# Sixteen small VectorE operations for f, layer-one roots behind the sine, a new priority table and last adds on GpSimd in a two-layer state-space kernel

## The chip, the cores and the metric

The kernel runs on one core of a Trainium2 chip. The metric is device microseconds (us) of one execution. Times are medians of several executions. A ratio is the mean time of one kernel's runs over the mean of the other's runs of the same rounds, so it is not quite the ratio of the medians that stand beside it. Each run of an altered kernel was timed beside fresh runs of the kernel before on the same chip; those medians lay between 357.3 and 358.5 us.

## The reference, cut to what matters

```python
x = A_x                                   # 2048 tokens x 640
for layer in (1, 2):                      # the same weights both times
    x = x + A(layernorm(x))               # diagonal complex recurrence h = lam*h + B u, y = 2 Re(C h) + D u
    x = x + B(layernorm(x))               # layernorm(x) times a long convolution of k and v (by FFT in the reference)
```

In A, `lam = exp(dt * Lambda)` and `B_bar = f * B` with `f = (lam - 1) / Lambda`, all complex, 640 states. The B term's convolution depends on k, v and fixed weights alone, so it can be computed at any time before it is used.

## The kernel before: the parts that the argument touches

The 2048 tokens are worked in four chunks of 512; a chunk has four quarters of 128 tokens ("q"). A layer-A chunk passes layernorm (its root is on ScalarE), products (`bp`), a rotation by a table of sines and cosines (`ri`, VectorE), a scan, the rotation back (`ro`), and four large groups of products (`cp`), one for each quarter.

The program does not fix an order by hand. Each piece of work is a task with dependencies, an estimated duration and a rank from a table `WHEN`. A list scheduler in the program gives each engine, as soon as it is free, the ready task of lowest rank (for some tasks the second number says how long to wait for the first choice of engine), and the instructions are then emitted in that planned sequence. Each engine runs its sequence strictly in order, so a planned order that does not fit the real durations shows up as waiting. The plan is made anew for every program.

The sine table of the rotation, and who must be done before it:

```python
B = (aw["tab"][...first 640*5 elements...], aw["W1"][:, 0])   # B's real part lies in the table's memory
...
t_m = S.add(f"a_gm{k}", "pe", ..., [t_dd] + w0s + bms, e_gm)     # five products that read B; gms = all five
...
def e_t1(_):                                                     # ScalarE: the table
    nc.scalar.activation(aw["tab"][:, 2], st["r"], ACT.Sin, ...)
    nc.scalar.activation(ab, st["r"], ACT.Abs)
    nc.scalar.activation(aw["tab"][:, 1], ab, ACT.Sin, ...)
    for j in range(NJ):
        nc.scalar.activation(aw["rtab"][:, j, :], st["it"], ACT.Identity, scale=0.0, bias=...)
t_t1 = S.add("a_t1", "act", 6.7, [t_t0] + gms, e_t1)             # so the sine waits for gms
```

The layer-one roots (in `bn_stats`) and the end of layer B in its last chunk, a group per quarter:

```python
t_sd = S.add(name + "_sd", "act", ..., [t_bn], e_sd)             # Sqrt: another activation table than Sin
...
# last chunk, one quarter q:
e_u:  b = (x + nmean) * Y          # one fused VectorE operation; needs only the mean
e_m:  Y = b * rstd + x             # one fused VectorE operation; needs the root
# other chunks: e_u normalizes (ScalarE or VectorE), one product over four quarters, four adds on VectorE
```

Of the kernel before, what the change touches and what calls it, by code (L numbers as in the profile page):

```python
# [9 lines left out]
ALU = mybir.AluOpType  # L10
# [7 lines left out]
P = 128  # L18
L = 2048
D = 640  # L20
# [32 lines left out]
    "warm": -5, "yt_io0": 2.55, "yt_ph0": 4.27, "yt_sin0": 5.89, "yt_neg0": 9.88, "yt_io6": 132.6, "yt_ph6": 8.2, "yt_sin6": 9.91, "yt_neg6": 13.01,  # L53
    "yt_io12": 8.8, "yt_ph12": 11.54, "yt_sin12": 13.59, "yt_neg12": 16.53, "yt_Ci": 21.14, "yt_Si": 22.8, "yt_nsi": 30.27, "yt_f0": 1.22, "yt_f2": 6.07,
    "yt_f3": 8.4, "yt_f4": 9.65, "yt_h0": 0.07, "yt_h1": 0.97, "yt_h2": 5.13, "yt_h3": 9.63, "kv_dsl": 1.97, "kv_kd": 2.73, "kv_k0": 13.36, "kv_k1":
    14.32, "kv_k2": 14.97, "kv_d0": 5.67, "kv_d1": 6.57, "kv_d2": 10.23, "kv_ds0": 10.65, "kv_lk0": -0, "kv_lv0": 9.8, "kv_mm0:0": 12.25, "kv_ev0:0":
    15.4, "kv_mm0:1": 15.02, "kv_ev0:1": 17.2, "kv_st0": 21.1, "kv_ds1": 13.44, "kv_lk1": 12.55, "kv_lv1": 15, "kv_mm1:0": 21.79, "kv_ev1:0": 25.02,
    "kv_mm1:1": 20.06, "kv_ev1:1": 22.17, "kv_st1": 32.7, "kv_ds2": 18.01, "kv_lk2": 35.6, "kv_lv2": 40.3, "kv_mm2:0": 48.16, "kv_ev2:0": 52.03,
    "kv_mm2:1": 40.92, "kv_ev2:1": 50.79, "kv_st2": 54.8, "kv_ds3": 30.92, "kv_lk3": 47.3, "kv_lv3": 43.8, "kv_mm3:0": 54.17, "kv_ev3:0": 56.25,
    "kv_mm3:1": 57.88, "kv_ev3:1": 59.99, "kv_st3": 76.1, "kv_ds4": 55.32, "kv_lk4": 68.7, "kv_lv4": 72.6, "kv_mm4:0": 78.97, "kv_ev4:0": 81.57,  # L60
    "kv_mm4:1": 72.36, "kv_ev4:1": 77.61, "kv_st4": 85.5, "a_pl": 0.17, "a_p0": 11.24, "a_p1": 13.98, "a_p2": 14.63, "a_p3": 15.78, "a_p4": 18.43, "a_p5":
    20.56, "a_p6": 23.36, "a_lamd": 23.86, "a_f": 28.37, "a_dd": 16.07, "a_ldB0": 2.4, "a_ldB1": 7.4, "a_wl00:0": 34.4, "a_wl00:1": 31.5, "a_wc00:0":
    37.93, "a_wm00:0": 39.1, "a_wc00:1": 40.53, "a_wm00:1": 40.04, "a_wl01:0": 40.21, "a_wl01:1": 37.9, "a_wc01:0": 42.58, "a_wm01:0": 49.98, "a_wc01:1":
    51.1, "a_wm01:1": 53.25, "a_wl02:0": 46.1, "a_wl02:1": 42.6, "a_wc02:0": 48.69, "a_wm02:0": 54.03, "a_wc02:1": 55.37, "a_wm02:1": 58.88, "a_wl03:0":
    71.4, "a_wl03:1": 56.5, "a_wc03:0": 74.94, "a_wm03:0": 75.97, "a_wc03:1": 76.97, "a_wm03:1": 79.87, "a_wl04:0": 65.2, "a_wl04:1": 74.9, "a_wc04:0":
    78.59, "a_wm04:0": 80.65, "a_wc04:1": 81.65, "a_wm04:1": 82.89, "a_b00:0": 9.82, "a_b0e0:0": (10.51, 0), "a_b00:1": 8.06, "a_b0e0:1": (9.33, 3),
    "a_b00:2": 11.53, "a_b0e0:2": (13.01, 1.5), "a_b00:3": 10.63, "a_b0e0:3": (12.42, -1), "a_b00:4": 7.7, "a_b0e0:4": (8.75, 3), "a_b01:0": 49.89,
    "a_b0e1:0": (50.52, 3), "a_b01:1": 14.62, "a_b0e1:1": (17.28, 0.8), "a_b01:2": 23.8, "a_b0e1:2": (24.94, 3), "a_b01:3": 18.33, "a_b0e1:3": (19.59,
    -1), "a_b01:4": 23.52, "a_b0e1:4": (24.36, 1.5), "a_b10:0": 33.92, "a_b1e0:0": (35, 3), "a_b10:1": 32.55, "a_b1e0:1": (33.68, 0), "a_b10:2": 25.31,
    "a_b1e0:2": (26.42, -1), "a_b10:3": 29.77, "a_b1e0:3": (31.02, 0), "a_b10:4": 26.8, "a_b1e0:4": (28.17, 3), "a_b11:0": 42.65, "a_b1e1:0": (43.58, -1),  # L70
    "a_b11:1": 28.31, "a_b1e1:1": (29.65, -1), "a_b11:2": 34.63, "a_b1e1:2": (35.54, -1), "a_b11:3": 46.77, "a_b1e1:3": (48.11, 99), "a_b11:4": 30.56,
    "a_b1e1:4": (31.47, -1), "a_gm0": 84.5, "a_ge0": (87.86, -1), "a_gm1": 87.84, "a_ge1": 90.96, "a_gm2": 104.18, "a_ge2": (107.4, 0), "a_gm3": 98.47,
    "a_ge3": (115.43, 1.5), "a_gm4": 92.78, "a_ge4": 96.07, "a_wl10:0": 97.9, "a_wl10:1": 89.8, "a_wc10:0": 115.48, "a_wm10:0": 107.45, "a_wc10:1":
    111.58, "a_wm10:1": 112.92, "a_wl11:0": 101.84, "a_wl11:1": 103.04, "a_wc11:0": 106.68, "a_wm11:0": 109.36, "a_wc11:1": 121.12, "a_wm11:1": 122.95,
    "a_wl12:0": 116.24, "a_wl12:1": 117.44, "a_wc12:0": 121.91, "a_wm12:0": 132.45, "a_wc12:1": 135.94, "a_wm12:1": 138.06, "a_wl13:0": 131.59,
    "a_wl13:1": 130.39, "a_wc13:0": 137.56, "a_wm13:0": 138.85, "a_wc13:1": 139.99, "a_wm13:1": 141.05, "a_wl14:0": 144.12, "a_wl14:1": 142.92,
    "a_wc14:0": 148.92, "a_wm14:0": 150.68, "a_wc14:1": 153.82, "a_wm14:1": 157.45, "a_ti": 20.17, "a_ta": 22.96, "a_t0": 26.17, "a_t1": 122.82, "a_t2":
    131.25, "yq0_kl": 4.8, "yq0_ka": 15.17, "yq0_KA:m0": 16.75, "yq0_KA:e0": (18.76, -1), "yq0_KA:m1": 19.31, "yq0_KA:e1": 20.32, "yq0_KA:m2": 17.03,
    "yq0_KA:e2": (17.86, -1), "yq0_KA:m3": 18.61, "yq0_KA:e3": (19.66, 99), "yq0_KB:m0": 25.89, "yq0_KB:e0": (27.01, 99), "yq0_KB:m1": 27.38, "yq0_KB:e1":
    (28.75, 0.8), "yq0_KB:m2": 24.08, "yq0_KB:e2": (25.52, 1.5), "yq0_KB:m3": 28.87, "yq0_KB:e3": (30.31, 0), "yq0_KB:m4": 26.57, "yq0_KB:e4": 27.91,  # L80
    "yq0_vl": 26.3, "yq0_VA:m0": 31.92, "yq0_VA:e0": (32.55, 0), "yq0_VA:m1": 31.61, "yq0_VA:e1": (32.24, 6), "yq0_VA:m2": 32.27, "yq0_VA:e2": (33.15,
    0.8), "yq0_VA:m3": 33.47, "yq0_VA:e3": (34.1, 99), "yq0_VB:m0": 35.91, "yq0_VB:e0": 36.98, "yq0_VB:m1": 37.48, "yq0_VB:e1": (38.73, 99), "yq0_VB:m2":
    36.58, "yq0_VB:e2": (37.97, 0), "yq0_VB:m3": 38.79, "yq0_VB:e3": (41.58, 0), "yq0_VB:m4": 40.18, "yq0_VB:e4": (39.51, 1.5), "yq1_kl": 28.99, "yq1_ka":
    34.59, "yq1_KA:m0": 39.9, "yq1_KA:e0": (41.76, 1.5), "yq1_KA:m1": 35.29, "yq1_KA:e1": (35.98, 6), "yq1_KA:m2": 35.57, "yq1_KA:e2": 36.58, "yq1_KA:m3":
    38.6, "yq1_KA:e3": (39.71, 0.8), "yq1_KB:m0": 43.29, "yq1_KB:e0": (44.32, 3), "yq1_KB:m1": 45.76, "yq1_KB:e1": (47.02, 0), "yq1_KB:m2": 44.86,
    "yq1_KB:e2": 46.12, "yq1_KB:m3": 43.97, "yq1_KB:e3": 45.22, "yq1_KB:m4": 47.51, "yq1_KB:e4": 49.78, "yq0_pw": 42.46, "yq0_IB:m0": 52.34, "yq0_IB:e0":
    53.78, "yq0_IB:m1": 51.44, "yq0_IB:e1": (52.78, 99), "yq0_IB:m2": 50.27, "yq0_IB:e2": (51.82, 0), "yq0_IB:m3": 53.95, "yq0_IB:e3": (54.47, 3),
    "yq0_IB:m4": 53.05, "yq0_IB:e4": 54.88, "yq0_tt": 64.47, "yq1_vl": 49.69, "yq1_VA:m0": 56, "yq1_VA:e0": (56.63, -1), "yq1_VA:m1": 57.69, "yq1_VA:e1":
    (58.43, 3), "yq1_VA:m2": 56.43, "yq1_VA:e2": (57.53, 3), "yq1_VA:m3": 56.75, "yq1_VA:e3": (57.6, -1), "yq1_VB:m0": 59.7, "yq1_VB:e0": 60.79,
    "yq1_VB:m1": 61.49, "yq1_VB:e1": (62.75, 0.8), "yq1_VB:m2": 60.37, "yq1_VB:e2": (61.69, 0.8), "yq1_VB:m3": 62.39, "yq1_VB:e3": 63.65, "yq1_VB:m4":  # L90
    61.27, "yq1_VB:e4": (62.15, -1), "yq0_IA:m0": 65.54, "yq0_IA:e0": (66.37, 6), "yq0_IA:m1": 66.03, "yq0_IA:e1": (67.27, 0.8), "yq0_st": 69.05,
    "yq2_kl": 52.2, "yq2_ka": 58.65, "yq2_KA:m0": 64.22, "yq2_KA:e0": (65.38, -1), "yq2_KA:m1": 63.55, "yq2_KA:e1": (64.19, -1), "yq2_KA:m2": 64.8,
    "yq2_KA:e2": (65.43, -1), "yq2_KA:m3": 63.86, "yq2_KA:e3": (64.49, 6), "yq2_KB:m0": 68.05, "yq2_KB:e0": (69.33, 99), "yq2_KB:m1": 66.86, "yq2_KB:e1":
    (68.17, 1.5), "yq2_KB:m2": 68.73, "yq2_KB:e2": (70.23, 0.8), "yq2_KB:m3": 69.62, "yq2_KB:e3": (71.13, 1.5), "yq2_KB:m4": 67.83, "yq2_KB:e4": (69.07,
    1.5), "yq1_pw": 66.59, "yq1_IB:m0": 78.02, "yq1_IB:e0": (79.4, -1), "yq1_IB:m1": 74.47, "yq1_IB:e1": (75.77, 0), "yq1_IB:m2": 76.21, "yq1_IB:e2":
    (77.78, 0.8), "yq1_IB:m3": 77.12, "yq1_IB:e3": (78.82, -1), "yq1_IB:m4": 75.54, "yq1_IB:e4": (76.67, 3), "yq1_tt": 80.49, "yq2_vl": 64.11,
    "yq2_VA:m0": 74.09, "yq2_VA:e0": (74.72, 0), "yq2_VA:m1": 71.61, "yq2_VA:e1": 72.94, "yq2_VA:m2": 71.25, "yq2_VA:e2": (73.84, 3), "yq2_VA:m3": 70.96,
# [312 lines left out]
def a_setup_tasks(S, nc, wp, St, consts, t_go, A_Lambda_re, A_Lambda_im, A_B_re, A_B_im, A_C_re, A_C_im, A_log_dt, A_Dskip, after_sin):  # L410
# [240 lines left out]
    def e_t2(_):  # L651
# [5 lines left out]
        v.tensor_scalar(aw["ctab"][:, 2, :], st["sn"][:, 1, :], -1.0, None, ALU.mult)  # L657

    T["tab"] = [S.add("a_t2", "dve", 1.2, [t_t1], e_t2)]

    T["w"] = w0s + w1s + gs
    return aw, T, t

# [879 lines left out]
```

## Time and profile before

| | kernel before |
|---|---|
| median | 358.4 us |
| profiled span | 356.8 us |
| TensorE busy, VectorE busy, ScalarE busy | 327.5, 315.1, 256.4 us |
| TensorE idle before its last product (345.7 us) | 18.2 us, of it 17.1 before 142 us |
| from TensorE's last product to the end | 11.1 us |
| stretches at half the TensorE clock before its end | one, 36.8 to 40.3 us |

The trace's clock records give TensorE's granted clock in stretches that are multiples of 3.41 us; the clock takes the values 1.0 and 0.5. ScalarE in order of time (start, length, engine, line, operation, then out and in), in the kernel before:

```profile
102.85 1.28 ACT L712 ACT_TABLE_LOAD   x1
104.15 0.30 ACT L712 ACTIVATE std<-mv,eps 128x4 f32<-128x4 f32 x1
...
107.94 0.92 ACT L726 ACTIVATE b<-b,nmr,rstd 128x640 bf16<-128x640 bf16 x1
...
126.65 1.28 ACT L644 ACT_TABLE_LOAD   x1
...
131.83 2.11 ACT L648 ACTIVATE rtab<-b,s_r 128x258 f32<-128x258 f32 x5
```

Chunk 0's root is at 104 us. The table with its load holds ScalarE from 126.65 to 133.85.

### The profile page before, as it was taken

What the parts mean: (1) busy time and instruction counts of PE and PEld (TensorE: products, weight loads), DVE (VectorE), ACT (ScalarE), POOL (GpSimd) and SP (SyncE); (2) the same over time, 40 slices, a digit from 0 to 9 for tenths busy, and PEclk for the clock granted to TensorE, in tenths of its full rate; (3) what the DMA queues carried; (4) which work ended last, traced back from release to release, by engine and by line L of the source; (5) the groups of instructions that cost most, each with busy time, mean ns of one, the idle gap of its engine ahead of it and who ended that gap; (6) DMA issues with size and microseconds to landing.
All of it is one profiled execution on the core that took longest, in us unless ns stands there. A gap on an engine that the chain in (4) does not pass through costs nothing.

```text
span 356.8 us, 8409 instructions
## 1 busy us (share of the span) xinstructions
PE 327.5 (92%) x3534; PEld 247.6 (69%) x3565; DVE 315.1 (88%) x479; ACT 256.4 (72%) x406; POOL 20.8 (6%) x51
## 2 busy tenths in 40 slices
PE   7686998989998997999999999999999999999970
PEld 7346876867686986986685677686866767755640
DVE  8799798798799797999999969979999679999896
ACT  3999798898799999943378599797256577306850
POOL 5841003000000000000000000000000000000000
PEclk9999899999999999999999999999999999999996
DMA  7999999999999982790226690605032022220141
GB/s 193 208 235 188 182 184 217 193 186 202 237 245 163 184 174 46 144 233 2 62 73 119 137 333 34 147 18 132 0 68 81 3 16 59 75 75 2 50 172 73
DMA packets 118712, 45.91 MB, mean 129 GB/s; under 512 B 111629, under 2 KB 112914, under 8 KB 118674
## 3 DMA queue, kind: packets, MB, share of 16 engines
q1 hardware_dynamic: 118528, 45.36, 59.9%
q8 instruction: 28, 0.46, 0.5%
q14 instruction: 10, 0.08, 0.1%
q10 hardware_dynamic: 146, 0.01, 0.0%
HBM read 17.38 MB, written 7.86 MB: 71 GB/s over the span
## 4 chain that ended last, share of the span: by engine, by line
PE 69%; ACT 10%; DVE 8%; DMA 7%; issue 3%; SPq 2%; DVEq 0%; ACTq 0%
PE ps L859 31%; PE ps L770 11%; PE ps L773 11%; ACT b L382 6%; PE ps L608 3%; PE ps L1163 3%; DMA b<-in_A_C_im_dram 2%; DMA b<-in_B_v_dram 2%; DVE b L1169 2%; PE ps L1313 2%; DMA b<-b 2%; PE ps L1314 1%; PE ps L1208 1%; SPq L536 1%; DMA b<-in_B_k_dram 1%
## 5 line engine op out<-in xcount | busy, mean ns | idle before, releaser
L382 ACT ACTIVATE b<-ps 128x1024 bf16<-128x1024 f32 (+3 forms) x125 | 109.6, 945 | 29.5 <-PE ps L773 25.5
L859 PEld LDWEIGHTS <-b 128*128 128x128 bf16 x880 | 67.7, 98 | 48.3
L859 PE MATMUL ps<-W,b 128*128 128x128 bf16 (+1 forms) x629 | 95.7, 298 | 0.6
L770 PE MATMUL ps<-b,BT 128*128 128x256 bf16 x400 | 56.8, 273 | 0.0
L773 PE MATMUL ps<-b,BT 128*128 128x256 bf16 x400 | 56.7, 273 | 0.0
L808 DVE TENSOR_TENSOR_SCAN b<-rtab,b 128x1290 bf16<-128x1290 f32 x16 | 44.7, 2833 | 0.3
L773 PEld LDWEIGHTS <-BT 128*128 128x128 bf16 x400 | 39.1, 98 | 4.5
L770 PEld LDWEIGHTS <-BT 128*128 128x128 bf16 x400 | 38.6, 98 | 4.4
L726 ACT ACTIVATE b<-b,nmr,rstd 128x640 bf16<-128x640 f32 (+1 forms) x43 | 37.0, 915 | 6.2 <-DVE nmr L693 6.2
L681 ACT ACTIVATE junk<-b,nmean 128x640 bf16<-128x640 f32 x48 | 39.7, 828 | 1.5
L1232 PE MATMUL ps<-b,b 128*128 128x128 bf16 x170 | 35.1, 219 | 1.2 <-ACT G L382 0.7
L1235 PE MATMUL ps<-b,b 128*128 128x128 bf16 x170 | 35.4, 219 | 0.0
L1237 PE MATMUL ps<-b,b 128*128 128x128 bf16 x150 | 32.8, 219 | 0.0
L1234 PE MATMUL ps<-b,b 128*128 128x128 bf16 x150 | 32.8, 219 | 0.0
L384 DVE CAST b<-ps 128x1024 bf16<-128x1024 f32 (+2 forms) x24 | 26.2, 1109 | 6.3 <-PE ps L1208 2.7
L867 ACT ACTIVATE b<-ps 128x640 f32<-128x640 f32 x16 | 11.1, 697 | 22.8 <-PE ps L859 22.8
L859 PE MATMUL ps<-G,b 128*128 128x128 bf16 (+1 forms) x152 | 26.5, 295 | 0.4
L1163 PE MATMUL ps<-b,fd 128*128 128x512 bf16 x73 | 18.6, 380 | 3.8 <-POOL fd L1141 2.0
L1313 PE MATMUL ps<-b,b 128*128 128x128 bf16 x160 | 19.4, 219 | 2.6 <-ACT b L382 2.1
L1314 PE MATMUL ps<-b,b 128*128 128x128 bf16 x160 | 19.2, 219 | 0.0
L552 ACT ACTIVATE b<-b,s_F 128x640 f32<-128x640 bf16 x20 | 17.2, 859 | 1.8 <-DVE W L556 1.4
L556 DVE SCALAR_TENSOR_TENSOR W<-b,s_F 128x640 bf16<-128x640 bf16 x20 | 17.4, 882 | 1.0 <-ACT b L552 0.7
(210 smaller groups left out, 560.3 us busy)
## 6 DMA issues: line engine op xcount, KB each, us to landing
b<-in_A_x_dram SPq DMA_DIRECT2D x8, 640.0 KB, 4.9
b<-ysd SPq DMA_DIRECT2D x8, 640.0 KB, 5.1
b<-in_B_ssm_k_dram SPq DMA_DIRECT2D x5, 512.0 KB, 8.6
kvd<-b SPq DMA_DIRECT2D x5, 512.0 KB, 4.3
b<-kvd SPq DMA_DIRECT2D x5, 512.0 KB, 5.4
ysd<-b SPq DMA_DIRECT2D x5, 512.0 KB, 5.0
out_dram<-b SPq DMA_DIRECT2D x8, 320.0 KB, 2.2
tab<-in_A_B_re_dram SPq DMA_DIRECT2D x1, 800.0 KB, 7.4
```

What stands on the lines that cost most here:

```text
L382: nc.scalar.activation(out, in_, ACT.Copy)
L681: nc.scalar.activation(small.junk, src(q), ACT.Square, bias=st["nmean"][:, i:i + 1], scale=1.0, accum_out=st["ssq"][:, i:i + 1])
L726: nc.scalar.activation(dst, src, ACT.Identity, bias=st["nmr"][:, i:i + 1], scale=st["rstd"][:, i:i + 1])
L770: nc.tensor.matmul(pb[:, jj, c2, :], lhsT=aw["BT1"][:, c2, j, k, :], rhs=uT[:, 0:2, k, :], start=(k == 0), stop=False)
L773: nc.tensor.matmul(pb[:, jj, c2, :], lhsT=aw["BT0"][:, c2, k, j * P:(j + 1) * P], rhs=uT[:, 2:4, k, :], start=False, stop=(k == NJ - 1))
L808: nc.vector.tensor_tensor_scan(gv, rt, gv, 0.0, ALU.mult, ALU.add)
L859: nc.tensor.matmul(pc[:, o0:o1], lhsT=lh, rhs=rh, start=(n == 0), stop=(n == len(ops) - 1))
L1163: nc.tensor.matmul(pk[:, 512 * b:512 * (b + 1)], lhsT=s_ds.get()[:, l, :], rhs=kT[:, t0:t0 + 512], start=(l == 0), stop=(l == 3))
L1232: nc.tensor.matmul(ps[:, g, 0, :], lhsT=T["Cf"].get()[:, q, :], rhs=are, start=True, stop=single)
L1234: nc.tensor.matmul(ps[:, g, 0, :], lhsT=T["Sf"].get()[:, q, :], rhs=A[:, 2 * q + 1, :], start=False, stop=True)
L1235: nc.tensor.matmul(ps[:, g, 1, :], lhsT=T["NSf"].get()[:, q, :], rhs=are, start=True, stop=single)
L1237: nc.tensor.matmul(ps[:, g, 1, :], lhsT=T["Cf"].get()[:, q, :], rhs=A[:, 2 * q + 1, :], start=False, stop=True)
```

## The change

Its intent: fewer tiny dependent operations for f; one activation-table load fewer for the roots and none for the sine, by making the roots follow the sine; a tail in which GpSimd and ScalarE take work from VectorE; and a new priority table for all of that. Cut to its core:

```diff
 WHEN = {
-    (862 ranks)
+    (every one of them new)
 }
@@ f: 25 small VectorE operations become 16 on pairs of planes; lam is stored as (-im, re, im)
@@ the table and the layer-one roots
+    T["t1"] = [t_t1]
-def bn_stats(S, nc, small, src, x_ready, name, uses):
+def bn_stats(S, nc, small, src, x_ready, name, uses, after):          # after = T["t1"]
-    t_sd = S.add(name + "_sd", "act", ..., [t_bn], e_sd)
+    t_sd = S.add(name + "_sd", "act", ..., [t_bn] + after, e_sd)
@@ layer B, last chunk
-            if len(qs) == 1:                 # every quarter in the fused form
+            if qs[0] == 3:                   # only quarter 3 in the fused form
...
+                    engs, ests = (("dve", "pool"), (0.77, 1.4)) if out is not None and c >= NCH - 2 else ...   # adds on either engine
+        if len(groups) > 1:                  # a store per quarter in the last chunk
```

## The prediction

> **What bounds the kernel now.** I read the page's busy row first, then the busy time by stretch, then the chain of waits and the order of time in the last stretch.
>
> The busy row has TensorE at 92% of 356.8 us and VectorE at 88%. Such shares are averages, so I cut the span where the behaviour changes. The columns are the stretch, its length, busy us (instructions) of TensorE, its weight loads, VectorE, ScalarE and GpSimd, then the granted clock, the DMA share and GB/s.
>
> ```profile
> 0.00:30.00 30.00, 22.02 (x240) 16.61 (x243) 25.16 (x71) 24.25 (x38) 17.83 (x45) 1.00 0.98 212
> 30.00:60.00 30.00, 27.43 (x395) 22.75 (x395) 25.94 (x48) 26.68 (x36) 2.94 (x6) 0.94 1.04 196
> 60.00:100.00 40.00, 37.28 (x559) 28.91 (x562) 32.38 (x33) 34.08 (x41) 0.00 (x0) 1.00 1.10 210
> 100.00:142.00 42.00, 38.16 (x550) 33.00 (x549) 36.47 (x74) 41.47 (x54) 0.00 (x0) 1.00 0.90 154
> 142.00:345.80 203.80, 202.65 (x1803) 146.35 (x1820) 187.43 (x244) 128.52 (x237) 0.00 (x0) 1.00 0.35 86
> 345.80:357.00 11.20, 0.00 (x0) 0.00 (x0) 7.69 (x13) 1.42 (x4) 0.00 (x0) 0.73 0.29 117
> ```
>
> There are three regimes. A head, 0 to 142 us, in which TensorE idles 8.0 + 2.6 + 2.7 + 3.8 = 17.1 us; in its last 42 us ScalarE is busy for 41.5, so the head ends ScalarE-bound. A body of 203.8 us in which TensorE idles only 1.2 us: it sets the pace and nothing else matters. A tail of 11.0 us, 345.8 to the span's end at 356.8, without any TensorE work. The change removes no matrix product, so it can gain only from those 17.1 us and those 11.0 us.
>
> The tail in order of time (start, length, what):
>
> ```profile
> 345.89 0.81 DVE L871 SCALAR_TENSOR_TENSOR b<-ps,b 128x640 f32<-128x640 f32 x1
> 346.63 0.88 DVE L901 SCALAR_TENSOR_TENSOR b<-b,nmean,b 128x640 bf16<-128x640 f32 x1
> 346.75 0.20 ACT L676 ACTIVATE nmean<-sums 128x1 f32<-128x1 f32 x1 [2.74 <-DVE b L871]
> 346.99 0.83 ACT L681 ACTIVATE junk<-b,nmean 128x640 bf16<-128x640 f32 x1
> 347.55 0.89 DVE L905 SCALAR_TENSOR_TENSOR b<-b,rstd,b 128x640 bf16<-128x640 bf16 x1
> 347.72 0.19 ACT L681 ACTIVATION_READ_ACCUMULATOR junk<-b,nmean 128x1 f32 x1
> 347.94 0.29 ACT L686 ACTIVATE std<-ssq,eps 128x1 f32<-128x1 f32 x1
> 348.35 2.47 DVE L901 SCALAR_TENSOR_TENSOR b<-b,nmean,b 128x640 bf16<-128x640 f32 x3
> 350.86 1.68 DVE L905 SCALAR_TENSOR_TENSOR b<-b,rstd,b 128x640 bf16<-128x640 bf16 x2
> 352.45 0.16 DVE L691 RECIPROCAL rstd<-std 128x1 f32<-128x1 f32 x1
> ...
> 352.72 0.88 DVE L905 SCALAR_TENSOR_TENSOR b<-b,rstd,b 128x640 bf16<-128x640 bf16 x1
> ```
>
> ScalarE has the root of the last quarter at 348.23, but VectorE takes up its reciprocal only at 352.45: for 4.2 us the last quarter waits behind work of other quarters. VectorE's backlog sets the end, not the dependency. After 353.6 there remain 3.2 us of output store.
>
> ScalarE's part of the head, as the page's group shows it: roots (L712) and the table's sine (L644) evict each other's activation table.
>
> ```profile
> L712 ACT ACT_TABLE_LOAD  x2: 1283/1283/1283, 102.9 to 134.9; - x2
> L644 ACT ACT_TABLE_LOAD  x1: 1283/1283/1283, 126.7 to 126.7; - x1
> ```
>
> So: load, two roots, load, sine, load, remaining roots. And one group about GpSimd (ns min/median/max):
>
> ```profile
> L1141 POOL TENSOR_TENSOR fd<-ident_bf,skf x20: 392/394/2311, 12.5 to 55.7; 128x128 bf16<-128x128 bf16 x20
> L487 DVE TENSOR_TENSOR b<-ident_bf,s_lam x1: 2311/2311/2311, 25.5 to 25.5; 128x1920 bf16<-128x1920 bf16 x1
> ```
>
> A 394 ns GpSimd product once took 2311 ns, exactly the length of the VectorE product beside it.
>
> **What the Trainium skill says.** (1) "ScalarE: Activation LUTs", What ACT_TABLE_LOAD costs: about 1283 ns per switch plus a drain of about 1380. The trace agrees on 1283; the drain does not show (the load starts at 102.85, the root behind it at 104.15), so I count 1.28. (2) "SBUF — State Buffer", Who interferes with whom: a VectorE instruction with two SBUF inputs and a GpSimd instruction that reads SBUF exclude each other for the whole instruction. The 2311 ns above agrees. (3) "GPSIMD Engine Reference", 3.1 Elementwise: about 2.6 cycles per element for two inputs, at 1.2 GHz 2.17 ns. With the trace's 394 ns for 128 columns the fixed part is 394 - 277 = 117, so 640 columns give an estimate of 1.5 us, against 0.77 on VectorE. No run shows that form yet. (4) "DMA: Bandwidth & Descriptors", Anatomy of one DMA: a fixed 2 us, mostly the receipt. The 320 KB output stores land after 2.2 us, so halving one saves little.
>
> **The change, part by part.**
>
> *f.* I count 25 operations before (lines 496 to 525), not 29, and 16 after. They run from 31.12 to 34.26 us: a dependent step costs 0.20 us, an independent one about 0.08. The new sequence has nine dependent steps and six others: 9 x 0.20 + 6 x 0.08 = 2.3 against 3.1, so 0.8 us of VectorE. Its first reader is the weight scaling at 42.2 us, 8 us later: slack, and of the 0.8 us I give the end 0.1. The new order of lam has the same three operations: 0.
>
> *Roots behind the sine.* One root load in place of two, and the sine's own falls away since the last set loaded is the sine's: 2 x 1.28 = 2.6 us less on ScalarE between 100 and 142 us, where it is full. The ceiling is TensorE's idle time there, 3.8 us. TensorE has other work to take up (the other layer's transforms), and the first two chunks' roots, at 104 and 108 us before, now wait for the table, which waits for all five products of the setup. I expect under half to arrive: 1.0.
>
> *The order.* Nearly every priority is new. Both loads of B now come first, and four of the five B_im transposes move from later into the first stretch, where TensorE idles 8 us. Five products of 128 columns at the trace's 0.056 us spacing make 0.28 us each, 1.1 for four. But the first kv product then starts later, behind 1.6 MB of B. I give this 0.4.
>
> *Tail.* Before, between 337.85 and 353.6 us, VectorE runs nearly without a gap. Concerned are four adds of chunk 2 (0.77 each) and, for quarters 0 to 2 of chunk 3, two fused operations (0.82 + 0.85): 3.1 + 5.0 = 8.1 us. After: a product per quarter, from 1.49 us for four quarters about 0.45; a normalization, on ScalarE or 0.57 on VectorE; an add, on either of VectorE and GpSimd. My choice: four of seven adds on GpSimd, two of three normalizations on ScalarE. VectorE keeps 3 x 0.77 + 3 x 0.45 + 0.57 = 4.2, a relief of 3.9 us. Against it the exclusion: four adds of 1.5 us on GpSimd, each able to hold up a two-input VectorE operation for part of its length; I take 0.4 us each, 1.6 back. Net 2.3. The floor: the last quarter's own chain (root out at 348.23, reciprocal, product with 1/std and add to 349.5, store 3.1) would end at 352.6, which caps the gain at 4.2. The last store is 160 KB in place of 320: 0.1.
>
> Sum: 0.1 + 1.0 + 0.4 + 2.3 + 0.1 = 3.9 us. From the median 358.4 that is 354.5.
>
> **The rivals.** *The GpSimd adds give back what they take.* For it: the 2311 ns record, and that GpSimd is twice slower by the estimate. If all four meet a two-input VectorE operation, 2.8 us come back, and a last add on GpSimd at 1.5 us could itself be last. Tail gain about 1, time 356.3. Against it: accumulating reads from PSUM[...] have one SBUF input and pass freely, and the very last quarter keeps its VectorE form. *The head is bound by DMA.* The DMA share is 0.9 to 1.1 up to 142 us and the chain there contains transposes of C and of the activations (3 to 5 us each); then freeing ScalarE moves nothing, and the later roots delay the first chunk: head gain -1 to 0, time about 356. Against it: ScalarE has hardly a gap from 110 to 142 us. *The new order is much better.* If it closes half of the head's 17.1 us besides the tail, 358.4 - 8 - 3 = 347. Against it: 6 to 8 us of that idle time are start-up and dependencies that no order removes, and the kernel was already tuned the same way.
>
> **Range and chances.** From -0.8 (both pessimistic rivals) to -7 (the tail at its cap and 3 us from the head): 351.5 to 357.6 at 8 in 10. Faster by over 2% means below 351.2, that is 7.2 us: the cap of 4.2 and 3 us from the head: 0.11. Slower by over 2% needs a new long wait in the body: 0.02. Within: 0.87.
>
> **What would show it.** One L712 table load and none at L644, four loads in all instead of six. TensorE idle in the body still about 1 us; if it is 3 or more, the new order has cost something and I am wrong there. The distance from TensorE's last product to the end: 8.6 us in place of 11.0; if still about 11, look at GpSimd adds above 1.5 us and VectorE operations stretched beside them. TensorE's last product near 344.3 in place of 345.7; if it is unchanged, the head's gain was an illusion, and if below 342, I undervalued the order.

## The result, and the profile after

| | before | after |
|---|---|---|
| median | 358.51 us (4 runs, 358.19 to 359.01) | 381.60 us (4 runs, 380.71 to 382.58) |
| ratio | | 1.064, 95% interval 1.061 to 1.067 |
| profiled span, mean clock | 356.8, 0.987 | 379.5, 0.964 |
| TensorE's last product ends | 345.7 | 368.6 |
| from there to the end | 11.1 | 10.9 |
| activation-table loads | 6 | 4 |

The table loads are as intended, and the tail is as long as it was. All the loss, 22.9 us, is before TensorE's last product. The busy time by stretch of the kernel after (columns as in the prediction):

```profile
100.00:142.00 42.00, 35.45 (x528) 30.17 (x527) 36.99 (x55) 38.20 (x48) 0.00 (x0) 0.92 0.78 152
142.00:368.70 226.70, 215.97 (x1912) 155.06 (x1909) 191.15 (x250) 129.33 (x237) 1.07 (x1) 0.98 0.33 79
```

The body, which had no gaps, now has 226.7 - 216.0 = 10.7 us of idle TensorE, and the clock column is below 1.00 in both stretches. The trace's clock records show the halved clock in five places before TensorE's end: at 14, 120, 134 and 253 us for 3.4 us each and at 349 us for 6.8 (before: one, 36.8 to 40.3 us).

That gives a first account of the 22.9 us. TensorE idles 30.3 us before its end against 18.2. (The trace of before lacks 31 of 3565 product records. Each missing one leaves a hole of 0.05 us that counts as idle, 1.6 us in all, which is also its body's 1.2 us: in traces of the same body with every record the body's idle time is 0.0. So the true difference is 13.7.) In the halved stretches TensorE was busy for 15.8 us against 3.4; half of that is lost, 7.9 against 1.7, so 6.2. About 3 us remain that I cannot divide between the two. This is bookkeeping of one trace, not what would be saved if one of the terms went away; the section on the price of a gap comes back to that.

The second account says where. Every kernel in the table below issues the same 3565 weight loads, so the time of the n-th load, minus the same in the kernel before, is TensorE's lag at that progress. (The order of products differs between kernels, so a lag within the first 230 us is good to some 3 us only: that of e1 moves between 5.6 and 8.5 from 160 to 205 us, where its TensorE has no gap of 0.1 us. Loads are counted from 0.) The later experiments are in the same table:

| weight load number | before, us | after | e2: order only | e3: roots only | e4: order and roots | e1: after without roots' wait |
|---|---|---|---|---|---|---|
| 750 | 67.6 | +0.8 | +2.0 | +0.6 | +2.9 | +0.3 |
| 1200 | 100.1 | +5.3 | +8.1 | +0.6 | +9.5 | +5.1 |
| 1500 | 120.3 | +7.0 | +8.7 | +8.3 | +11.8 | +7.9 |
| 1950 | 159.7 | +6.5 | +8.2 | +11.8 | +10.8 | +8.5 |
| 2700 | 240.1 | +9.4 | +8.2 | +12.1 | +13.9 | +8.5 |
| 2850 | 257.7 | +14.7 | +7.6 | +12.1 | +19.2 | +8.0 |
| 3450 | 331.1 | +14.4 | +8.2 | +12.1 | +19.0 | +8.5 |
| 3564 (last) | 345.4 | +22.9 | +8.2 | +12.1 | +28.3 | +8.5 |

Three steps in the kernel after: some 9 us in the head, 5 us near 250 us, 8 us near 350 us. What TensorE waited for in its body, in us in total, times, and the longest:

```profile
PE ps L851 <- DVE b L825: 7.7, 2, 7.0
PE ps L851 <- ACT b L384: 2.4, 1, 2.4
```

These are the last two steps: the products `cp` (L851) waiting for VectorE's rotation (L825) and for an eviction on ScalarE. For the 7.0 us, VectorE's work in order of time:

```profile
337.38 1.49 DVE L915 TENSOR_TENSOR b<-b,b 128x2560 bf16<-128x2560 bf16 x1
338.89 3.03 DVE L923 TENSOR_TENSOR b<-b,b 128x640 bf16<-128x640 bf16 x4
...
342.30 5.58 DVE L800 TENSOR_TENSOR_SCAN b<-rtab,b 128x1290 bf16<-128x1290 f32 x2
...
351.47 1.50 DVE L825 TENSOR_TENSOR b<-b 128x2580 bf16<-128x2580 bf16 x1
```

VectorE is full, but it does layer B2's chunk 1 (product and four adds, 4.5 us, needed only for an output) before the scan that TensorE's last chunk of work hangs on. The first step is in the head; there ScalarE reads:

```profile
107.20 1.32 ACT L635 ACTIVATE tab<-b 128x1290 bf16<-128x1290 f32 x1
...
113.25 1.28 ACT L704 ACT_TABLE_LOAD   x1
114.55 0.30 ACT L704 ACTIVATE std<-mv,eps 128x4 f32<-128x4 f32 x1
...
117.25 0.93 ACT L718 ACTIVATE b<-b,nmr,rstd 128x640 bf16<-128x640 bf16 x1
```

The table is now early and the roots come behind it: chunk 0's root starts at 114.55 where it started at 104.15, and its first normalization on ScalarE at 117.25 where it started at 107.94. But 5.3 us of lag are there already at the 1200th load, at 105 us, before any of this; e1 below shows what else the first step holds.

The tail, VectorE and GpSimd:

```profile
367.63 4.83 POOL L923 TENSOR_TENSOR b<-b,b 128x640 bf16<-128x640 bf16 x3 [306.06 <-DMA out_dram<-b]
...
369.43 3.72 DVE L923 TENSOR_TENSOR b<-b,b 128x640 bf16<-128x640 bf16 x2
```

Two VectorE adds took 3.72 us beside GpSimd's three (the prediction had assumed four on GpSimd); two such adds in a row take 1.56 us alone (e5, at 335.81). That stretch of 2.2 us is on the chain that ended last.

### The profile page after: what moved, and what is told of

It reads as the page before. It is cut to its first block, busy times and chain, and to the rows that moved or that the text cites. A ratio compares the mean times of both kernels' runs of the same rounds, so it can differ in the third digit from the quotient of the medians. Undisturbed runs are those within 1.5% of the kernel's fastest.

```text
span 379.5 us, 8447 instructions
## 1 busy us (share of the span) xinstructions
PE 338.3 (89%) x3565; PEld 251.5 (66%) x3565; DVE 317.2 (84%) x474; ACT 252.1 (66%) x400; POOL 24.0 (6%) x54
## 5 line engine op out<-in xcount | busy, mean ns | idle before, releaser
L384 ACT ACTIVATE b<-ps 128x1024 bf16<-128x1024 f32 (+3 forms) x121 | 106.2, 946 | 25.7 <-PE ps L765 18.8
L851 PEld LDWEIGHTS <-b 128*128 128x128 bf16 x880 | 68.5, 99 | 61.2 <-DVE b L825 8.0
L851 PE MATMUL ps<-W,b 128*128 128x128 bf16 (+1 forms) x640 | 99.4, 305 | 10.1 <-DVE b L825 7.7
L718 ACT ACTIVATE b<-b,nmr,rstd 128x640 bf16<-128x640 f32 (+1 forms) x46 | 39.7, 911 | 28.0 <-DVE nmr L685 26.6
L1232 PE MATMUL ps<-b,b 128*128 128x128 bf16 x170 | 35.9, 224 | 4.0 <-ACT b L384 3.9
L386 DVE CAST b<-ps 128x1024 bf16<-128x1024 f32 (+2 forms) x28 | 29.1, 1059 | 11.9 <-PE ps L1237 6.0
L1235 PE MATMUL ps<-b,b 128*128 128x128 bf16 x170 | 36.1, 223 | 0.0
L1237 PE MATMUL ps<-b,b 128*128 128x128 bf16 x150 | 33.6, 224 | 0.0
L1234 PE MATMUL ps<-b,b 128*128 128x128 bf16 x150 | 33.6, 224 | 0.0
L851 PE MATMUL ps<-G,b 128*128 128x512 bf16 (+1 forms) x160 | 27.0, 299 | 0.0
L668 ACT ACTIVATE nmean<-sums 128x4 f32<-128x4 f32 (+1 forms) x15 | 3.0, 202 | 35.5 <-DVE b L863 25.5
L1163 PE MATMUL ps<-b,fd 128*128 128x512 bf16 x80 | 20.3, 397 | 4.5 <-ACT b L384 1.6
L923 POOL TENSOR_TENSOR b<-b,b 128x640 bf16<-128x640 bf16 x3 | 4.8, 1638 | 306.1 <-DMA out_dram<-b 306.1
L1313 PE MATMUL ps<-b,b 128*128 128x128 bf16 x160 | 19.1, 219 | 0.9 <-DVE b L386 0.6
L1208 PE MATMUL ps<-FA,b 64*128 64x128 bf16 x320 | 14.8, 223 | 5.1 <-ACT b L384 3.8
```

Of the source, the lines that this page charges most:

```text
L384: nc.scalar.activation(out, in_, ACT.Copy)
L386: nc.vector.tensor_copy(out, in_)
L718: nc.scalar.activation(dst, src, ACT.Identity, bias=st["nmr"][:, i:i + 1], scale=st["rstd"][:, i:i + 1])
L851: nc.tensor.matmul(pc[:, o0:o1], lhsT=lh, rhs=rh, start=(n == 0), stop=(n == len(ops) - 1))
L1232: nc.tensor.matmul(ps[:, g, 0, :], lhsT=T["Cf"].get()[:, q, :], rhs=are, start=True, stop=single)
L1234: nc.tensor.matmul(ps[:, g, 0, :], lhsT=T["Sf"].get()[:, q, :], rhs=A[:, 2 * q + 1, :], start=False, stop=True)
```

## The experiments

The theories at the start. **R**: the wait of the roots makes the first chunk late, and the new ranks then run the rest out of step. **O**: the new priority table is bad by itself. **G**: the GpSimd adds cost it. Beside them **C**: each gap is paid a second time by the halved clock.

### The parts one by one: e1 to e4

e1 is the changed kernel without the roots' wait:

```diff
-    t_sd = S.add(name + "_sd", "act", ..., [t_bn] + after, e_sd)
+    t_sd = S.add(name + "_sd", "act", ..., [t_bn], e_sd)
```

> The changed kernel with only the added dependency taken out (the layer-one roots no longer wait for the table's sine); new order, GpSimd adds, short f all kept. Theory R (the wait makes the first chunk's roots late, and the priority table then runs the rest out of step): the three steps in TensorE's lag vanish, TensorE ends near 344 to 346, time 350 to 357 us, and the table loads are five or six again. Theory O (the new priority table itself is bad): still above 370. Theory G (the GpSimd adds cost it): still above 375, since they are kept.

Measured: 366.43 us, ratio 1.025 (1.020 to 1.030), six table loads. Better than the changed kernel by 14 us, and still slower than before. It is none of the three numbers expected. R as stated is half right: both late steps are gone (last column of the table above), the first stays. So the first step of the changed kernel is not owed to the wait of the roots.

e2 is the kernel before with the new ranks and nothing else.

> The kernel before with the new priority table and nothing else. Theory R: 355 to 361, the table alone is harmless. Theory O: above 370, with TensorE idle in the body above 8 us.

Measured: 368.17 us, ratio 1.030 (1.027 to 1.034). Neither theory's number: the table is not harmless, and not the whole loss. Its lag of 8 us is complete by the 1500th load, so it is an affair of the head, and the body adds nothing. In the trace TensorE idles 22.0 us before its end against 18.2, and loses 6.2 us to halved stretches (at 12, 36, 87 and 121 us) against 1.7: 3.8 + 4.5 = 8.3 of the 8.2. The tail is 12.4 us in place of 11.1. What TensorE waited for between 60 and 130 us, in e2:

```profile
PE ps L1945 <- ACT b L1119: 3.1, 5, 1.4
PE ps L1945 <- DVE b L1121: 1.6, 1, 1.6
```

and the same line of the program in the kernel before:

```profile
PE ps L1208 <- ACT b L382: 1.4, 4, 0.5
PE ps L1208 <- DVE b L1169: 0.6, 1, 0.6
```

These are the first products of the transforms, waiting for ScalarE or VectorE, mostly to copy earlier results out of PSUM: 4.7 us in place of 2.0. I did not find which ranks do it.

e3 is the kernel before, in its old order, with the roots' wait. The table's rank is the new, earlier one, and its estimated duration the new 5.5 in place of 6.7.

```diff
-    "a_t1": 122.82, "a_t2": 131.25,
+    "a_t1": 101.91, "a_t2": 108.08,
-    ... [t_bn], e_sd)
+    ... [t_bn] + after, e_sd)
```

> The kernel before with its old priority table plus the roots' wait alone (the table's sine given the new, earlier priority, so that the wait is as short as it can be). Theory R in its strong form (the wait costs 20 us wherever it is): above 375. Theory R with an interaction (wait and new table together): 358 to 368. Theory O: 358 to 362. Four table loads in all either way.

Measured: 370.75 us, ratio 1.037 (1.033 to 1.042), four table loads. That lies between the two forms of R (above 375, or 358 to 368) and above what O allows, so the wait is dear without any help from the new order. The lag is 0.6 us up to the 1200th load and 11.8 at the 1950th. ScalarE there:

```profile
111.05 1.26 ACT L1381 ACTIVATE tab<-b 128x1290 bf16<-128x1290 f32 x1
...
117.04 1.28 ACT L1450 ACT_TABLE_LOAD   x1
118.34 0.48 ACT L1450 ACTIVATE std<-mv,eps 128x4 f32<-128x4 f32 x2
```

The table starts at 111 us; the last of the five products ends at 110.5. From 111.05 to 118.7 ScalarE does table, load and roots in one piece, and copies nothing out of PSUM. TensorE idles 10.3 us between 100 and 142 us (3.8 before). The early table alone does not do it in the new order: e2 has it at 110 us too, without the wait and with chunk 0's root at 100.79, and TensorE idles 3.6 us in that stretch. What was to save 2.6 us of ScalarE moved the roots from 104 to 118 us.

e4 has both, without f and without the tail.

> The kernel before with the new priority table and the roots' wait, without the tail's split and GpSimd adds and without the short f. If these two make the whole loss: 380 to 386, as slow as the changed kernel plus the gain of the tail that is missing. If the tail's GpSimd adds make part of it: below 376.

Measured: 387.24 us, ratio 1.083 (1.079 to 1.087). The two together make the whole loss and more: 10.9 (e2) and 13.4 (e3) add to 24.3, e4 costs 29.9. In the head their losses overlap, and in return the two late steps at 250 and 350 us appear, which neither shows alone. The 5.6 us by which e4 is slower than the changed kernel are not explained. They arise in the head, before any of the tail's work: at the 2700th load e4's lag is 13.9 us, and 9.4, 8.3 and 7.6 in the changed kernel, e9 and e17. Of the change's parts only the short f acts there, so with this order and this wait f, or the new plan that comes with it, may be worth several us; no run tests it.

### Tail and f: e5 to e7, e10, e17

e5 is the kernel before with the tail alone (split groups, adds on either engine, a store per quarter, and five new ranks for the new tasks); e6 the same with all adds on VectorE; e7 the short f alone. In e6:

```diff
-    engs, ests = (("dve", "pool"), (0.77, 1.4)) if out is not None and c >= NCH - 2 else ...
+    engs, ests = "dve", 0.83 if out is None else 0.77
```

> The kernel before with the tail's part alone: a product per quarter, normalization and add apart for quarters 0 to 2, adds of the last two chunks on either engine, a store per quarter; old order. If the tail's gain was rightly predicted (2.3 us): 354.5 to 356, and TensorE's end to the span's end 8.5 to 9.5 us in place of 11.1. If the GpSimd adds give back what they take: 356.5 to 358, distance about 11.

> As the run of the tail alone, but every add stays on VectorE. If GpSimd gains as predicted: slower than the tail alone by 1 to 2 us (356 to 358). If GpSimd's adds are too slow and hold VectorE up: equal or faster, 354 to 356.

> The kernel before with the short f and the new order of lam alone. The short f has 8 us of slack, so the same as before within 0.3%: 356.5 to 358.5. If the path to the first weights did run through f, up to 1 us faster.

Measured: e5 357.93 us (ratio 1.000, 0.998 to 1.001), e6 357.77 (1.000, 0.996 to 1.003), e7 358.04 (1.001, 0.996 to 1.006). The tail gains nothing with GpSimd or without, and f in the old order is the null that was predicted. Why the tail gains nothing stands in the last rows of e5:

```profile
351.24 0.92 ACT L1468 ACTIVATE b<-b,nmr,rstd 128x640 bf16<-128x640 f32 x1 [3.17 <-DVE nmr L1435]
352.19 0.49 DVE L1665 TENSOR_TENSOR b<-b,b 128x640 bf16<-128x640 bf16 x1 [0.99 <-ACT b L1468]
352.72 0.83 DVE L1673 TENSOR_TENSOR b<-b,b 128x640 bf16<-128x640 bf16 x1
```

The quarter that comes last goes the long way (reciprocal, ScalarE, product, add), and VectorE waits 0.99 us for ScalarE. The change keeps the short fused form for quarter 3, because in the new order TensorE finishes quarter 3 last. In the old order it is quarter 2. So e5 and e6 were not a fair trial; e10 fuses quarter 2, with all adds on VectorE:

```diff
-            if qs[0] == 3:
+            if qs[0] == 2:
```

> The kernel before with the tail's split, all adds on VectorE, and the quarter that keeps the fused form being the one that TensorE finishes last (quarter 2 in the old order; the change fuses quarter 3, which is last only in the new order). If the tail alone and its VectorE form gained nothing because the last quarter was normalized in the long form (reciprocal, ScalarE, product, add, with VectorE idle 1 us): TensorE's end to the span's end 8 to 9 us in place of 11.1, time 355 to 356.5. If the store or the number of stores bounds the tail: about 11 us and 358 again.

Measured: 356.74 us, ratio 0.995 (0.993 to 0.998); from TensorE's end to the span's end 9.6 us. Both are just outside the ranges expected for a gain, and clear of those for none. The last rows of VectorE:

```profile
350.74 0.16 DVE L1433 RECIPROCAL rstd<-std 128x1 f32<-128x1 f32 x1
...
351.01 0.88 DVE L1654 SCALAR_TENSOR_TENSOR b<-b,rstd,b 128x640 bf16<-128x640 bf16 x1
```

No wait is left and the last result is there at 351.9 us in place of 353.6. From there to the span's end it is 2.9 us in place of 3.2, here and in every trace with the smaller last store. The idea of the tail is worth 1.5 us, without GpSimd. For GpSimd in the order it was made for, e17 takes only its adds out of the changed kernel, by the edit of e6.

> The changed kernel with every add on VectorE, nothing else. TensorE's end unchanged (368 to 370). If the GpSimd adds give back what they take (three adds of 1.64 us there, while two VectorE adds beside them take 3.6 us in place of 1.56): within 1 us of the changed kernel, 380.5 to 382.5. If they gain the 2.3 us that was predicted of the tail: 383 to 385.

Measured: 381.92 us, ratio 1.066 (1.064 to 1.069), TensorE's last product at 368.0. GpSimd's adds are worth 0.3 us of 381.6, which is within the spread. Theory G is out, as a loss and as a gain.

### The wait for the five products: e8 and e13

If the roots' wait costs because the sine hangs on the five products, then a sine that need not wait for them should make it cheap. The products read B, whose real part lies in the sine's memory. e8 put four of the five rows of B's real part into what I took for the table's first plane, the fifth into a tile of its own, and let the sine run at once.

> The kernel before, old order, with the roots' wait kept but the cause of its length removed: the real part of B no longer lies in the memory of the table's sine, so the sine runs at about 30 us without waiting for the five products of the setup. If the wait costs because it hangs the first chunk's roots on the five products: 355 to 361, against 370.8 with the wait as shipped, three or four table loads, and TensorE idle between 100 and 142 us back near 4 us from 10. If the roots' place itself or anything else about the dependency costs: above 366.

Measured: 361.62 us, ratio 1.010, four table loads, TensorE idle 3.2 us between 100 and 142 us. That is 0.6 us above the range expected if the products are the cause. But **the result was wrong**: a plane has 1290 elements and four rows of B have 2560, so the sine overwrote part of B before its last reader. The time nearly fits, the kernel does not count. e13 does it rightly, with B's real part in a half of the second weight buffer that nothing else writes before the five products are done (the table's two ranks, 100 and 109, are not in this cut):

```diff
-    B = (aw["tab"][...first 640*5 elements...], aw["W1"][:, 0])
+    B = (aw["W1"][:, 1], aw["W1"][:, 0])
-    t_t1 = S.add("a_t1", "act", 6.7, [t_t0] + gms, e_t1)
+    t_t1 = S.add("a_t1", "act", 5.5, [t_t0], e_t1)
```

> The kernel before, old order, with the roots' wait kept, B's real part moved into the half of the second weight buffer that nothing writes before the five products are done, and so the sine free to run at about 30 us. If the wait costs because of the five products: 356 to 361 with a correct result (370.8 with the wait as shipped), four table loads or fewer, TensorE idle between 100 and 142 us at most 4.5 us against 10.3. If the dependency itself costs: above 366.

The sine in its trace:

```profile
33.53 1.32 ACT L1381 ACTIVATE tab<-b 128x1290 bf16<-128x1290 f32 x1
```

Measured: correct, 362.29 us, ratio 1.008 (1.004 to 1.012), four table loads, TensorE idle 2.8 us between 100 and 142 us. The wait as shipped cost 13.4 us; freed of the products it costs some 3.8 by the medians, 2.9 by the ratio of means, just outside what I expected. So the products are the cause of most of it. Two table loads saved do not pay for the remainder. Part of that may be the table at 33 us, where ScalarE has other work: TensorE idles 4.1 us between 30 and 60 us against 2.6 before. No run separates it.

The six runs of e13 show something else. They took 358.5, 359.2, 361.9, 362.7, 362.8 and 362.8 us, with mean granted clocks of 0.991, 0.981, 0.976, 0.969, 0.969 and 0.969. One program, and here the time follows the clock. It is not a rule for all of them: e7's four runs took 356.5, 357.7, 358.4 and 360.4 us at 0.978, 0.979, 0.979 and 0.984, the longest at the highest clock. Only one run of a kernel has a trace, so where the others lost their time is not on record.

### VectorE's order at 340 us: e9

The changed kernel, with five ranks altered so that the scan comes before the product and adds of B2's chunk 1:

```diff
-    "B2c1_mm": 281.11, "B2c1_m:0": 285.53, "B2c1_m:1": 304.2, "B2c1_m:2": 282.79, "B2c1_m:3": 283.18,
+    "B2c1_mm": 330, "B2c1_m:0": 330.1, "B2c1_m:1": 330.2, "B2c1_m:2": 330.3, "B2c1_m:3": 330.4,
```

> The changed kernel with five priorities altered: the output product and the four adds of layer B2's chunk 1 come after the scan and the rotation of layer A2's chunk 3 on VectorE instead of before them. If the last of the three steps in TensorE's lag (about 8 us of 22.9) is VectorE doing the wrong work first: the 7.0 us gap before TensorE's last chunk shrinks to 2.5 us or less, its halved window goes, TensorE ends 5 to 7 us earlier, time 374 to 377. If VectorE is simply behind there, whatever its order: 380 or more.

Measured: 376.63 us, ratio 1.053 (1.051 to 1.054). As expected; VectorE, in order of time, and what TensorE waited for between 330 and 362 us:

```profile
336.79 5.58 DVE L1540 TENSOR_TENSOR_SCAN b<-rtab,b 128x1290 bf16<-128x1290 f32 x2
...
345.96 1.50 DVE L1565 TENSOR_TENSOR b<-b 128x2580 bf16<-128x2580 bf16 x1
```

```profile
PE ps L1591 <- DVE b L1565: 2.6, 1, 2.6
```

The scan starts 5.5 us earlier, the wait at the end of the body is 2.6 us in place of 7.0, no halved stretch follows it, and TensorE ends at 361.8, 6.8 us earlier. At the 3450th load it was 1.0 us ahead (lag 13.4 against 14.4), so this step shrank by 5.8, from 8.5 to 2.7. Of the 6.8 us, 1.4 come back in the tail (12.3 us), into which VectorE has carried the postponed work.

### The price of a gap: e11 and e12

Theory C, tested where nothing else happens: TensorE's body in the kernel before. A group `cp` starts with a product on a small tile z, GpSimd then fills z, and a second product waits for that. e11 has 8 such pauses of seven fills, e12 has 24 of one fill.

```diff
+                if f"{nm}_cp:{q}" in PAUSED:
+                    nc.tensor.matmul(pc[:, 896:1024], lhsT=z[:, 0:P], rhs=z[:, 0:P], start=True, stop=True)
+                    for _ in range(7):                     # 1 in e12
+                        nc.gpsimd.memset(z[:], 0.0)
+                    nc.tensor.matmul(pc[:, 896:1024], lhsT=z[:, 0:P], rhs=z[:, 0:P], start=True, stop=True)
```

> The kernel before with 8 pauses put into TensorE's full body: TensorE waits for seven small GpSimd memsets, about 2 to 4 us each (correct results, the extra products go to unused columns). If a half-idle clock window is paid for by a halved one: the trace shows about 5 to 8 new halved windows of 3.41 us, and the time rises by the sum of the pauses plus about 1.7 us for each halved window. If the clock is only a coincidence: it rises by the pauses alone and no halved window appears in the body.

> The kernel before with 24 short pauses in TensorE's body (one GpSimd memset each, about 0.7 to 1.2 us), spread one per product group so that no 3.41 us window is half idle. Clock theory: no halved window in the body, and the time rises by no more than the sum of the pauses (24 x about 0.9 = 22 us). If any idle gap lowers the clock: halved windows here too, and a rise above the sum.

Measured: e11 420.06 us, ratio 1.174 (1.171 to 1.178); e12 385.08, ratio 1.075 (1.073 to 1.077). What TensorE waited for in e11, then the ten products after the first pause:

```profile
PE ps L854 <- POOL z L853: 40.6, 8, 5.4
```

```profile
193.22 4.18 PE L867 MATMUL ps<-W,b 128*128 128x512 bf16 x10
```

and in e12:

```profile
PE ps L854 <- POOL z L853: 19.4, 24, 0.8
```

```profile
194.41 2.32 PE L867 MATMUL ps<-W,b 128*128 128x512 bf16 x10
```

The same ten products take 2.32 us after a short pause and 4.18 after a long one. e12 has no halved stretch in the body and costs 27.0 us (385.08 - 358.09), 1.12 for a pause of 0.81: the other 0.31 are the two extra products and the refilling. e11 has one or two halved windows behind each pause, eight stretches in the body. It costs 62.0 us: the waits 40.6, the overhead 8 x 0.31 = 2.5, and half of the 37.6 us for which TensorE was busy at half clock, 18.8, together 61.9. Theory C stands for long pauses where TensorE sets the pace, but a gap is not paid twice: a pause of 5.1 us cost 7.7, half as much again. (The pauses were longer than the 2 to 4 us planned, and brought 15 halved windows, not 5 to 8. e12 is 5 us above its bound of the pauses alone: the overhead.)

When is a window halved? In all twenty traces I cut the full-speed time before TensorE's end into windows of 3.41 us, counted back from the halved stretch that ends it, and took TensorE's busy share in each, from 9 us on. 44 windows were the last before a halved stretch: in 42 of them the share was below 0.52, and the other two had 0.53 and 0.56. Of the 1912 windows that a full-speed window followed, seven had a share below 0.52. So about 1.7 us of idle time inside one window was followed by the half rate in 42 of 49 cases, in one gap or in several: the halved stretch at 120 us in the kernel after follows a window with four gaps of 0.2 to 0.5 us. It is no certainty: two of the seven lie in e9, with 0.43 and 0.47, around its waits at 345 and 249 us.

The bookkeeping of gaps and clock is not the same as what would be saved. The step at 250 us begins in the changed kernel, e9 and e17 with the same wait of 2.4 us. A halved stretch follows it in the changed kernel only, yet the step is 5.3, 5.1 and 5.2 us: in e9 and e17 TensorE, at full speed, soon waits again, 1.1 and some 0.7 to 0.9 us. And e17, with 13.7 us of halved stretches before TensorE's end where the changed kernel has 20.5, ends TensorE at 368.0 us against 368.6.

### Mends: e14 to e16, e18

e14 is e13 with the tail of e10.

> As the run before it in this call, with the tail split and the fused quarter last. The two gains should add: 1 to 2 us below that run. If it falls below 356.7 the early sine is worth keeping, otherwise the last-quarter version without it is the better kernel.

Measured: 360.88 us, ratio 1.007 (1.005 to 1.009). The median is 1.4 us below e13's, but the means differ by 0.4 and e13's runs by 4.3, so that the gains add is not shown. The early sine is not worth keeping.

e15 is the complete changed kernel with e13's memory for B and, for every task whose old rank is under 100, the old rank.

> The changed kernel complete, with the sine's memory mended as above and the old priorities for all tasks ranked before 100 us. If the changed kernel's loss is the head's order and the wait for the products: 354 to 360. If the rest of the new order loses as well: above 364.

Measured: 361.00 us, ratio 1.008 (1.006 to 1.010); TensorE's last product at 347.6, no gap above 0.3 us behind 142 us. That is between the two ranges expected. Of the 23.1 us lost, 20.6 are recovered, with the later ranks, GpSimd's adds, short f and roots behind the sine all kept. The late steps are absent without any cure of their own. The two edits, memory and early ranks, were not tried one by one in this kernel. e18 is e15 with the adds on VectorE.

> The mended changed kernel (e15) with every add on VectorE. If GpSimd's adds are neutral: 360 to 362. If they gain: 363 to 366. If they hold VectorE up on the last chain: 358 to 360.

Measured: 362.94 us (361.2 to 364.0), ratio 1.014 (1.010 to 1.018). Two of its four runs had a clock of 0.968, and the other two (361.2 and 362.0, at 0.983 and 0.987) lie on average 0.5 us above the mean of e15's four (0.979 to 0.988). So at equal clock GpSimd's adds gain 0.5 us at most by these few runs, within the spread of e15 (360.8 to 361.7); the 1.9 us between the medians are probably mostly clock.

e16 is e10 with 20 dummy products of 128 columns in front of the first kv product, where TensorE waits 1.4 us for GpSimd:

```diff
+                for i in range(20 if kb == 0 and h == 0 else 0):
+                    nc.tensor.matmul(pk[:, 0:P], lhsT=ident, rhs=ident, start=True, stop=True)   # overwritten by what follows
```

> The run with the fused last quarter, with 20 dummy products of 128 columns put in front of the first kv product, where TensorE waits 1.4 us for a diagonal of GpSimd. If the halved window at 13 to 16 us costs its 1.7 us at the end of the kernel: no halved window there in the trace, and 0.5 to 1.7 us below e10's 356.7. If the head has slack there: the same as e10 within 0.4 us.

Measured: 356.19 us, ratio 0.992 (0.990 to 0.994). The halved stretch at 13 us, which e10's trace has, is absent; but it is absent too from the traces of the kernel before, e5, e6, e11, e12 and e14, which have no dummy products, so one trace does not show that these did it. Four runs took 356.2 us and two 354.7; e10 took 355.0 and 356.6 to 357.2. By the medians a gain of about 0.5 us on e10, at the lower edge of what I expected, and within the spread of e10's runs. This is the fastest kernel, faster than both, by 0.8% over the kernel before.

## Why the prediction was wrong, by its own steps

Predicted 354.5 us, measured 381.6.

**What bounds the kernel** was read rightly: head, body and tail exist as described, and in the body every gap of TensorE counts. The sentence that fell is "can gain only from those 17.1 us and those 11.0 us", taken together with 0.02 for slower: the body has no slack to lose either, and I gave nothing for new gaps in it. The falsifier that I had named, idle TensorE in the body above 3 us, is what came.

**Roots behind the sine: +1.0 predicted, about -13 measured** (e3). The saving is real, six loads became four. The step that failed is "TensorE has other work to take up". I had seen that the roots now wait for the table, and the table for all five products, and did not work out when that is: in e3 the table starts at 111 us where the root had been at 104, with 6 us of table and a load before the roots, so that chunk 0's root moved by 14 us (10 in the changed kernel) and ScalarE copied nothing out of PSUM for 7.7 us. TensorE had not enough other work: it idled 10.3 us between 100 and 142 us in place of 3.8. In the changed kernel the wait costs as much (381.6 us against e1's 366.4) by another way, through the steps at 250 and 350 us. The rival "the later roots delay the first chunk" had the direction and -1 us at most. It needed one sum: the new start of the first root, minus the old.

**The order: +0.4 predicted, about -11 measured** (e2), of it 8.2 before TensorE's last product; about -9 with the short f and the tail it was made for (e1). The step that failed is taking every rank but a few as neutral: I credited what I could see (four transposes moved into idle time) and gave the other 800 no cost. What came was 8 us of lag in the head, where the transforms' first products waited 4.7 us in place of 2.0. From the ranks alone the loss could not be read, but it deserved a broad range, and none was given to the downside.

**Both together** made the steps at 250 and 350 us, which belong to neither part alone (e1 to e4). Being late alone does not make them: e1 and e3 are 8.5 and 12.1 us late and have neither. The one at 350 was VectorE's order (e9). Both are absent in e15, which keeps the later ranks and the roots behind the sine but takes the delay out of the head. What exactly makes the step at 250, which begins with a wait of 2.4 us for ScalarE, I have not settled.

**The clock** was no term of the prediction, although the clock column stood in its first view, at 0.94 for 30 to 60 us. By the bookkeeping it makes 6.2 of the 22.9 us and more than half of e2's loss at TensorE's end. That need not be what it caused, since at full clock TensorE can meet the next wait instead, as at 250 us. In e11, where nothing else waits, it makes 2.4 us of every long pause.

**Tail: +2.3 predicted; 0.2 in the changed kernel's tail (0.7 against e4, which has its order but the old tail), 0 in e5 and e6, 1.5 in e10.** The backlog argument was right in kind: with the proper quarter fused, VectorE works without a wait to the end and the distance falls. The term that was mis-sized is the mutual hold-up. An add on GpSimd that did not wait took 1.40 us (1.5 estimated), one that met VectorE adds up to 1.98, and the two VectorE adds beside GpSimd's three were stretched by 2.2 us, where I had allowed 1.6 for four. The rival "the GpSimd adds give back what they take" was right, as e17 shows.

**f: +0.1 predicted, 0.0 measured** in the old order (e7), right there; with the new order and the wait it stays open (e4). **The last store: +0.1 predicted**; from VectorE's last operation to the end it is 2.9 us in place of 3.2, so 0.3.

## What to carry to other kernels

Before moving an operation behind another to save a table load, work out the new start of the first thing that depends on it, along its whole chain of waits; a saving of 2.6 us on a busy engine is worth nothing if the first chunk starts 14 us later. A tuned priority table is tuned for its own dependencies and durations: change one dependency and the order must be judged anew, part by part, from a trace. Where TensorE sets the pace, count a long gap at more than its length (5.1 us cost 7.7 here); short ones that lie apart cost no clock (24 of 0.8 us, e12). Where something else is late as well, the lost clock may cost nothing, so test before mending it.

## What the Trainium skill lacked or had wrong

- "TensorE: Matmul & The Clock Gate", Part 1 and the table of "Why this matters for your kernels", has the window of 3413 ns and the half rate, and both agree with the clock records here. It gives the condition as one idle window and as no idle gap above some 3 us. Here a window whose busy share was below 0.52 was mostly enough (42 of 49 such windows), so 1.7 us of idle time in one window, even in four gaps of 0.2 to 0.5 us, can bring the half rate, and 2.6 us (e9) need not.
- The same page's cold and warm rates agree with ten 512-column products in 4.18 against 2.32 us. It tells of run-to-run differences for the cold start alone, and puts them below 1% of a kernel. Six runs of e13 went from 358.5 to 362.8 us, 1.2%, in step with mean clocks from 0.991 to 0.969; those of e7 were not in step.
- "ScalarE: Activation LUTs", What ACT_TABLE_LOAD costs: the 1283 ns agree, the drain of about 1380 does not show. In the kernel after, the load is issued at 113.25 us, when the work before it has ended, and the root follows at 114.55.
- "SBUF — State Buffer", Who interferes with whom: nothing wrong; two VectorE adds took 3.72 us beside GpSimd adds, 1.56 alone, while VectorE's operations that read PSUM took 0.82 us beside them as without.
- "GPSIMD Engine Reference", 3.1 Elementwise: 2.6 cycles per element led to an estimate of 1.5 us for 128x640; an add that did not wait for VectorE took 1.40, those that did up to 2.07 (e5).
